# Loading only the 96 rows with data of r, k and w, from the fifth unit on

## The chip, the cores and the metric

The kernel runs on one core of a Trainium2 chip. Its time is the device time of one execution in microseconds (us). The kernel before takes 333.74 us, the median of three runs (333.08 to 336.19).

## The reference

Two layers follow each other: a linear attention with a decaying state (4 batches, 8 heads, 768 steps, head width 48), and a mixture of eight experts of which each token uses one (3072 tokens of width 384, hidden width 1024).

```python
for t in range(S):
    cur = np.einsum('bhd,bhe->bhde', u[None] * kt, vt)
    y[:, :, t] = np.einsum('bhd,bhde->bhe', rt, state + cur)
    state = wt[:, :, :, None] * state + np.einsum('bhd,bhe->bhde', kt, vt)
...
e_idx = np.argmax(x @ w_gate + modality_bias[modality_id], axis=1)
...
h = np.maximum(x[mask] @ w1[e], 0.0)
out[mask] = gate_w[mask, None] * (h @ w2[e])
```

## The kernel before, in words

**Units.** The attention is cut into 24 units (4 batches times 6 chunks of 128 steps); unit n is one chunk with its eight heads. Four heads' r, k and w stand on 64 partitions and the other four on the next 64. A head is only 48 wide, so of each 64 rows 48 hold data and 16 are padding. The host lays the padding out as 0 for r and k and 1.0 for w, and until now it is loaded with the rest: line 99 moves 128 rows, w (517 numbers a row, 2068 bytes) as one transfer and r with k (1024 numbers, 4096 bytes) as a second one. They go into one of four buffers, `ins[n % 4]`, called in0 to in3 in the listings. v has its own transfer (line 102, 128 rows of 2304 bytes).

**The work on a unit.** VectorE forms running products of the decay with two scans over 516 columns, B (line 296) and E (line 299), and writes four columns of w anew (line 298). GpSimd forms K (line 246) and G (line 307) from k and r, ScalarE copies r to PSUM (line 240), half_v (line 262) prepares v, and TensorE makes the products. In step i of the loop, units i+2, i+1 and i are at different stages (`att_iter`, line 288), every engine has the order of its work written out by hand, and unit i+6 is loaded into the buffer that unit i+2 has just left: its w may go once E of unit i+2 is done, its r and k once G and the copy of r are done. Lines 178 to 180 load the routing bias (bb) and the modality ids (mi, mi2) early; bb is read by VectorE at line 192. Steps 4 to 7 load pieces of expert weights (raw, line 223), steps 8 to 11 clear rows of a scratch tensor (xs, line 873), each of about the size of v's load.

**Queue and semaphores.** All these transfers are issued by SP, one after another. They announce their landing on eight semaphores that are taken in turn, called DMAHW0 to DMAHW7 in the listings. Before a transfer is issued, SP waits until the transfer that had the semaphore last, the eighth before it, has landed. So SP never has more than eight transfers under way.

**After the attention** come six blocks of 512 (or 416) tokens and a smaller one through the experts; the change touches nothing there. Lines 667 and 744, which the prediction uses for comparison, move four transfers of 32 rows each for a block, into and out of the chip's memory.

Of the kernel before, what the change touches and what calls it, by code (L numbers as in the profile page):

```python
# [17 lines left out]
B, H, S, D = 4, 8, 768, 48  # L18
P = 128
# [41 lines left out]
def kernel(ctx: ExitStack, tc: tile.TileContext, rkw, vt, wf, cst, mid, wg, bias, w1, w2, out):  # L61
    nc = tc.nc
# [22 lines left out]
    NIN = 4  # L85
    ins = [pa.tile([P, 1600], F32, name=f"in{i}", bufs=1) for i in range(NIN)]
# [9 lines left out]

    def load(n, cuts=((0, 1541),)):
        for c0, c1 in cuts:
            nc.sync.dma_start(out=ins[n % NIN][:, c0:c1], in_=rkw[n, :, c0:c1])

    def loadv(n):
        nc.sync.dma_start(out=wt(n, "v", [P, VW], 4), in_=vt[n * P:(n + 1) * P, :])
# [4 lines left out]
    nc.vector.memset(wm, 0.0)  # L107
    cs = cp.tile([P, NCST], F32, name="cs")
    load(0, ((1024, 1541), (0, 1024)))
    load(1, ((1024, 1541),))  # L110
    nc.sync.dma_start(out=cs[:, 256:NCST], in_=cst[:, 256:NCST])
    loadv(0)
    load(1, ((0, 1024),))
    nc.gpsimd.memset(cs[:, 0:2 * P], 1.0)
    for c0, op in ((0, ALU.is_equal), (P, ALU.is_gt)):
# [720 lines left out]
    for i in range(-2, NU):  # L836
# [39 lines left out]
        if i == NU - 3:  # L876
# [5 lines left out]
                                       in_=zt[:, None, :].to_broadcast([P, JT, XW])))  # L882
# [299 lines left out]
```

## Time and profile before

| what | value |
|---|---|
| median of three runs | 333.74 us |
| the profiled execution itself | 332.86 us |
| its span, first to last instruction | 331.1 us |
| busy over the span: TensorE, VectorE, ScalarE, GpSimd | 97%, 67%, 62%, 59% |
| moved by DMA | 66.22 MB, on average 200 GB/s |

Busy time is a mean over stages with different limits. In the page's 40 slices of 8.3 us each, VectorE shows 9 or 8 tenths in most of the first 13 slices (the attention, up to about 110 us) and much less behind them, while TensorE shows 9 nearly everywhere. A line such as "<-DMA in<-rkw" behind an idle time names what ended that idle time.

### The profile page before, as it was taken

Reading aid. Unit: us, or ns where it says so; the run is one execution under the profiler, and the core shown is the slowest. Engines: PE = TensorE matmul, PEld = TensorE weight load, DVE = VectorE, ACT = ScalarE, POOL = GpSimd, SP = SyncE. Lnnn points to the kernel's source line nnn. Section 1 sums busy time; section 2 is a strip of 40 time slices with the busy share of each in tenths; the row PEclk is TensorE's granted clock in tenths of the full one; section 3 lists DMA queues with packets and bytes.
Section 4 is the critical chain, followed back from the end, with each engine's and each line's share of the span. In section 5 each row is a group of like instructions: output and inputs, shape, how many; then the busy total and the mean of one; then the engine's idle time right before and its main releaser. Section 6 shows DMA issues by size and latency. Waiting matters only on the chain. (4 is left out here: it accounts for less than half of the span.)

```text
span 331.1 us, 9946 instructions
## 1 busy us (share of the span) xinstructions
PE 319.8 (97%) x3831; PEld 279.6 (84%) x3831; DVE 222.0 (67%) x382; ACT 204.0 (62%) x466; POOL 195.0 (59%) x226
## 2 busy tenths in 40 slices
PE   8899999999899999999999999999999999999993
PEld 3688999889799897888888888888888999889993
DVE  6999999899999746777514995874472465353220
ACT  3898799677588875642314748637775786524240
POOL 7998889879999975575435550652056233604041
PEclk9999999999999999999999999999999999999999
DMA  7998889967998532514778128945996594332011
GB/s 267 414 332 263 272 295 258 302 229 246 303 287 277 183 97 89 104 72 173 238 236 213 51 69 201 375 144 131 325 259 262 146 342 157 78 104 78 0 70 56
DMA packets 48321, 66.22 MB, mean 200 GB/s; under 512 B 27569, under 2 KB 34825, under 8 KB 48264
## 3 DMA queue, kind: packets, MB, share of 16 engines
q1 hardware_dynamic: 45160, 56.02, 55.0%
q0 software_dynamic: 3104, 9.47, 7.4%
q8 instruction: 32, 0.52, 0.6%
q14 instruction: 25, 0.20, 0.2%
HBM read 61.65 MB, written 16.46 MB: 236 GB/s over the span
## 5 line engine op out<-in xcount | busy, mean ns | idle before, releaser
L760 POOL DMA_INDIRECT out<-ot,xg x24 | 25.3, 1054 | 72.2 <-ACT ot L772 67.7
L228 ACT CAST wh<-raw 128x768 fp32r<-128x768 f32 x48 | 39.0, 830 | 32.3 <-PE pK_d L730 16.3
L229 POOL TENSOR_TENSOR wl<-raw,wh 128x768 fp32r<-128x768 f32 x20 | 38.8, 1953 | 28.5 <-ACT wh L228 28.4
L717 DVE SCALAR_TENSOR_TENSOR h<-pS_u,h 128x512 fp32r<-128x512 f32 (+1 forms) x34 | 22.9, 674 | 36.1 <-ACT h L716 30.9
L229 DVE TENSOR_TENSOR wl<-raw,wh 128x768 fp32r<-128x768 f32 x28 | 31.0, 1113 | 15.2 <-ACT wh L228 14.5
L711 PE MATMUL pS_u<-xh,wh 128*128 128x512 f32 (+1 forms) x102 | 39.7, 390 | 0.2 <-DVE h L717 0.2
L711 PE MATMUL pS_u<-xo,wh 128*128 128x512 f32 (+1 forms) x102 | 39.2, 384 | 0.0
L711 PE MATMUL pS_u<-xh,wl 128*128 128x512 f32 (+1 forms) x102 | 39.1, 384 | 0.0
L716 ACT ACTIVATE h<-pS_u 128x512 fp32r<-128x512 f32 (+1 forms) x34 | 19.8, 582 | 26.6 <-PE pS_u L711 22.5
L641 POOL DMA_INDIRECT xs<-xp,posT x24 | 24.5, 1022 | 11.2 <-issue 8.2
L246 POOL TENSOR_TENSOR K<-in,B 128x512 f32<-128x512 f32 x24 | 28.4, 1185 | 4.2 <-PE pK L321 2.3
L307 POOL TENSOR_TENSOR G<-in 128x512 f32<-128x512 f32 x24 | 30.6, 1274 | 0.0
L730 PE MATMUL pY_d<-h,wh 128*128 128x512 f32 (+1 forms) x80 | 30.5, 381 | 0.0
L730 PE MATMUL pX_d<-h,wh 128*128 128x512 f32 (+1 forms) x80 | 30.5, 381 | 0.0
L730 PE MATMUL pK_d<-h,wh 128*128 128x512 f32 (+1 forms) x80 | 30.5, 381 | 0.0
L296 DVE TENSOR_TENSOR_SCAN B<-in,pX_d 128x516 f32<-128x516 f32 x24 | 29.3, 1220 | 1.8 <-DMA in<-rkw 1.8
L299 DVE TENSOR_TENSOR_SCAN E<-in,pX_d 128x516 f32<-128x516 f32 x24 | 29.5, 1229 | 0.8
L386 PE MATMUL pY<-v,A 128*64 128x48 f32 x368 | 25.1, 222 | 0.0
L348 DVE TENSOR_TENSOR A<-pS,m 128x768 f32<-128x768 f32 x24 | 22.8, 948 | 2.9 <-PE pS L346 2.7
L252 ACT ACTIVATE pU_st<-pU_st,B 128x48 f32<-128x48 f32 x80 | 22.0, 275 | 3.0 <-PE pU_st L358 0.5
L386 PEld LDWEIGHTS pY<-v,A 128*64 128x64 f32 x368 | 23.7, 138 | 0.0
L346 PEld LDWEIGHTS pS<-R,K 64*64 64x64 f32 x768 | 18.6, 133 | 5.1 <-issue 4.2
(248 smaller groups left out, 829.6 us busy)
## 6 DMA issues: line engine op xcount, KB each, us to landing
raw<-w SPq DMA_DIRECT2D x24, 768.0 KB
in<-rkw SPq DMA_DIRECT2D x23, 512.0 KB
v<-vt SPq DMA_DIRECT2D x24, 288.0 KB
in<-rkw SPq DMA_DIRECT2D x23, 258.5 KB
wg<-wf SPq DMA_DIRECT2D x8, 576.0 KB
xl<-xs SPq DMA_DIRECT2D x20, 192.0 KB
raw<-w SPq DMA_DIRECT2D x16, 192.0 KB
yd<-yt SPq DMA_DIRECT2D x16, 192.0 KB
```

The costliest lines, as they stand in the source:

```text
L228: nc.scalar.copy(out=wh[k][:, sl], in_=raw[k][:, sl])
L229: (eng or (nc.vector, nc.gpsimd)[k]).tensor_tensor(out=wl[k][:, sl], in0=raw[k][:, sl], in1=wh[k][:, sl].bitcast(F32), op=ALU.subtract)
L246: nc.gpsimd.tensor_tensor(out=wt(a, "K", [P, 4, P]), in0=quarters(k), in1=quarters(T["B", a][:, 1:517])[:, :, 1:129], op=ALU.mult)
L296: nc.vector.tensor_tensor_scan(out=Bt[:, 516:0:-1], data0=w[:, 516:0:-1], data1=d1[:, 516:0:-1], initial=0.0, op0=ALU.mult, op1=ALU.max)
L299: nc.vector.tensor_tensor_scan(out=Et, data0=w[:, 0:516], data1=d1[:, 1:2].to_broadcast([P, 516]), initial=1.0, op0=ALU.mult, op1=ALU.max)
L307: nc.gpsimd.tensor_tensor(out=wt(a, "G", [P, 512]), in0=r, in1=k, op=ALU.mult)
L386: nc.tensor.matmul(out=yh[64:P, g, sw, hh], lhsT=A[:, hh, g, 1 + sw], rhs=vs[:, g, hh] if sw else v[:, h * D:(h + 1) * D], start=new and n ...
L641: rows_apart("xs", nc.gpsimd.indirect_dma_start(out=xs[:, :], out_offset=bass.IndirectOffsetOnAxis(ap=posT[:, n:n + 1], axis=0), in_=T["xp ...
L711: nc.tensor.matmul(out=pp, lhsT=wsrc[0][:, f, c * P:(c + 1) * P], rhs=xsrc[:, c], start=(n == 0), stop=(n == 3 * KC - 1))
L717: nc.vector.scalar_tensor_tensor(out=hl, in0=pp, scalar=0.0, in1=hh.bitcast(F32), op0=ALU.max, op1=ALU.subtract)
L730: nc.tensor.matmul(out=X["y", q][c][:, 0:width(q)], lhsT=wsrc[1][:, f, c * P:(c + 1) * P], rhs=hsrc, start=(first and n == 0), stop=(last ...
L760: ins = nc.gpsimd.indirect_dma_start(out=out[:, :], out_offset=bass.IndirectOffsetOnAxis(ap=xg[0:n, j, 1:2].bitcast(I32), axis=0), in_=ot[ ...
```

## The change

Units 0 to 3 load as before, all 128 rows, so each of the four buffers gets its padding once. From unit 4 on only rows 0 to 47 and rows 64 to 111 are loaded, each range as a transfer of its own; the padding from the buffer's first unit stays there.

```diff
     def load(n, cuts=((0, 1541),)):
         for c0, c1 in cuts:
-            nc.sync.dma_start(out=ins[n % NIN][:, c0:c1], in_=rkw[n, :, c0:c1])
+            for q in (slice(0, P),) if n < NIN else (slice(0, D), slice(64, 64 + D)):
+                nc.sync.dma_start(out=ins[n % NIN][q, c0:c1], in_=rkw[n, q, c0:c1])
```

One line is added, so every later line's number grows by one. Line 99's two transfers for a unit become four for each of units 4 to 23. On SP, where units 4 to 6 are loaded, this stood before (the target, its source, rows x numbers a row, and the semaphores that SP waits for first):

```order
L99 DMA in0_94<-rkw 128x517 [waits DMAHW3_49,DVE_49]
L99 DMA in0_94<-rkw 128x1024 [waits DMAHW4_49,Activation_49,Pool_49]
L99 DMA in1_95<-rkw 128x517 [waits DMAHW5_49,DVE_49]
L99 DMA in1_95<-rkw 128x1024 [waits DMAHW6_49,Activation_49,Pool_49]
L102 DMA v3_363<-vt 128x576 [waits DMAHW7_49]
L99 DMA in2_96<-rkw 128x517 [waits DMAHW0_49,DVE_49]
L99 DMA in2_96<-rkw 128x1024 [waits DMAHW1_49,Activation_49,Pool_49]
L178 DMA bb_139<-bias 128x16 [waits DMAHW2_49]
L179 DMA mi_140<-mid 24x256 [waits DMAHW3_49]
L180 DMA mi2_163<-mid 24x256 [waits DMAHW4_49]
```

The first row is w of unit 4, the second its r and k. A transfer takes the semaphore that it waited for: w of unit 4 takes DMAHW3, and mi waits for its landing. In the changed kernel the same stretch reads:

```order
L100 DMA in0_94<-rkw 48x517 [waits DMAHW3_49,DVE_49]
L100 DMA in0_94<-rkw 48x517 [waits DMAHW4_49]
L100 DMA in0_94<-rkw 48x1024 [waits DMAHW5_49,Activation_49,Pool_49]
L100 DMA in0_94<-rkw 48x1024 [waits DMAHW6_49]
L100 DMA in1_95<-rkw 48x517 [waits DMAHW7_49,DVE_49]
L100 DMA in1_95<-rkw 48x517 [waits DMAHW0_49]
L100 DMA in1_95<-rkw 48x1024 [waits DMAHW1_49,Activation_49,Pool_49]
L100 DMA in1_95<-rkw 48x1024 [waits DMAHW2_49]
L103 DMA v3_367<-vt 128x576 [waits DMAHW3_49]
L100 DMA in2_96<-rkw 48x517 [waits DMAHW4_49,DVE_49]
L100 DMA in2_96<-rkw 48x517 [waits DMAHW5_49]
L100 DMA in2_96<-rkw 48x1024 [waits DMAHW6_49,Activation_49,Pool_49]
```

Eight semaphores now reach back over little more than one and a half units instead of nearly three. v3 waits for the first half of unit 4's w, and behind these rows bb waits for DMAHW0, the second half of unit 5's w.

On GpSimd, where K of unit 4 is made, the instruction waits for three semaphores before:

```order
L303 TENSOR_TENSOR dV2_480<-v2_199,dT2_434 128x384 [waits DMAHW2_49,Activation_49,Pool_49]
L246 TENSOR_TENSOR K4_482<-in0_94,B4_475 128x512 [waits DMAHW4_49,DVE_49,PE_49]
L307 TENSOR_TENSOR G4_484<-in0_94 128x512 [waits PE_49]
L421 TENSOR_TENSOR xp0_388<-xp0_388,dV1_382 128x384 [waits Activation_49]
L194 TENSOR_TENSOR ec_167<-ec_167,cs_100 128x16 [waits DMAHW3_49,DVE_49]
```

and for four in the changed kernel, one for each of the two transfers of r and k:

```order
L304 TENSOR_TENSOR dV2_488<-v2_199,dT2_440 128x384 [waits DMAHW2_49,Activation_49,Pool_49]
L247 TENSOR_TENSOR K4_490<-in0_94,B4_483 128x512 [waits DMAHW5_49,DMAHW6_49,DVE_49,PE_49]
L308 TENSOR_TENSOR G4_492<-in0_94 128x512 [waits PE_49]
L422 TENSOR_TENSOR xp0_394<-xp0_394,dV1_388 128x384 [waits Activation_49]
L195 TENSOR_TENSOR ec_167<-ec_167,cs_100 128x16 [waits DMAHW3_49,DVE_49]
```

The order of the work on GpSimd, ScalarE, VectorE and TensorE is otherwise the same; only the waits for r, k and w name two transfers where they named one.

## Rows read from the trace of the kernel before

**Rows 1.** Windows: stretch, its length, busy us by engine (instructions), clock, DMA share, GB/s.
```profile
5.00:20.00 15.00, 13.06 (x280) 9.93 (x278) 14.66 (x19) 11.56 (x36) 13.47 (x22) 1.00 1.03 400
20.00:110.00 90.00, 87.59 (x2252) 81.02 (x2250) 86.22 (x122) 71.92 (x220) 80.32 (x86) 1.00 0.86 273
```

**Rows 2.** Tile in: count, ns min/median/max, first and last start; idle ended by it (us, times).
```profile
L99 SPq DMA_DIRECT2D in<-rkw x47: 327/328/1282, 0.8 to 94.5; - x47
L296 DVE TENSOR_TENSOR_SCAN B<-in,pX_d x24: 1216/1219/1228, 3.7 to 108.2; 128x516 f32<-128x516 f32 x24
...
  DMA in<-rkw: 5.9, 4
```

**Rows 3.** Timeline of POOL: start, us, what, [idle before <-releaser].
```profile
8.52 1.19 POOL L246 TENSOR_TENSOR K<-in,B 128x512 f32<-128x512 f32 x1 [0.94 <-DMA in<-rkw]
```

**Rows 4.** DMA issues: line's transfer, queue, count, KB each.
```profile
in<-rkw SPq DMA_DIRECT2D x23, 512.0 KB
v<-vt SPq DMA_DIRECT2D x24, 288.0 KB
in<-rkw SPq DMA_DIRECT2D x23, 258.5 KB
raw<-w SPq DMA_DIRECT2D x16, 192.0 KB
```

**Rows 5.** Timeline of SP around unit 11's load.
```profile
36.25 0.33 SPq L99 DMA_DIRECT2D in<-rkw  x1
36.78 0.34 SPq L223 DMA_DIRECT2D raw<-w  x1
37.32 0.33 SPq L99 DMA_DIRECT2D in<-rkw  x1
```

**Rows 6.** Timeline of DVE: scan B of unit 11, which reads that load.
```profile
51.20 1.22 DVE L296 TENSOR_TENSOR_SCAN B<-in,pX_d 128x516 f32<-128x516 f32 x1
```

**Rows 7.** Waits of SP's queue: who waited, for whom, us, times, longest.
```profile
SPq L99 <- DVE E L299: 20.5, 17, 2.2
SPq L99 <- POOL G L307: 15.7, 13, 2.4
...
SPq L99 <- DMA in<-rkw: 1.5, 3, 0.8
```

**Rows 8.** Timeline of SP: issue of v3, mi, and unit 7's r and k.
```profile
11.34 0.44 SPq L102 DMA_DIRECT2D v<-vt  x1
...
16.46 0.44 SPq L179 DMA_DIRECT2D mi<-mid  x1
...
19.72 1.28 SPq L99 DMA_DIRECT2D in<-rkw  x1
```

**Rows 9.** Timelines of ACT and DVE: first readers of v3 and of bb.
```profile
22.27 0.72 ACT L262 COPY vz<-v 64x192 f32<-64x192 f32 x2
...
23.38 0.16 DVE L192 TENSOR_REDUCE emx<-bb 128x2 f32<-128x16 f32 x1
```

**Rows 10.** Timeline of SP: four 32-row loads, and four 32-row stores.
```profile
134.22 1.97 SPq L667 DMA_DIRECT2D xl<-xs  x4
...
161.96 2.04 SPq L744 DMA_DIRECT2D yd<-yt  x4
```

**Rows 11.** Windows of 0.25 us while those loads, then those stores, run.
```profile
136.25:136.50 0.25, 0.25 (x3) 0.21 (x2) 0.25 (x2) 0.13 (x1) 0.04 (x1) 1.00 1.06 283
163.00:163.25 0.25, 0.25 (x3) 0.19 (x2) 0.25 (x1) 0.00 (x0) 0.15 (x1) 1.00 0.89 212
```

**Rows 12.** Lines 246 and 240: wait instructions on the queues of POOL and ACT.
```profile
L246 POOLq EVENT_SEMAPHORE  x24: 17/1237/2517, 4.9 to 107.4; - x24
...
L240 ACTq EVENT_SEMAPHORE  x23: 17/38/38, 8.4 to 110.1; - x23
```

## The prediction, made before the changed kernel ran

> **What bounds the kernel now.** The change works between the first load of unit 4 and the last load at 94.5 us [rows 2], so I read the attention alone, first by windows. From 20 to 110 us VectorE is busy 86.22 of 90 us and TensorE 87.59; the DMA engines are 0.86 busy and move 273 GB/s [rows 1]. High shares on three sides do not say which one holds the others back, so the next view is what ended the idle times. Transfers of r, k and w ended four idle times, 5.9 us in all [rows 2], and the last of them ended at 8.52 us, before K of unit 1 [rows 3]. In the waits of 20 to 115 us no transfer stands. So no engine waits for a load that the change makes smaller; the compute engines set the pace, one unit every (108.2 - 3.7) / 23 = 4.54 us [rows 2], and the loads follow the buffers: SP's own long waits at line 99 are for E (20.5 us) and G (15.7 us) to release a buffer [rows 7].
>
> How far ahead the loads are is seen on unit 11. Its w is issued at 36.25 us and read at 51.20 us, 15 us later [rows 5, 6].
>
> The one stretch where DMA is scarce is 5 to 20 us, at share 1.03 and 400 GB/s [rows 1]. There the eight semaphores already bind: 1.5 us of SP's waits at line 99 are for the landing of r, k and w [rows 7]. That is where I look for harm.
>
> **The change part by part.**
>
> *Bytes removed.* 32 rows of 6164 bytes in 20 units are 3.95 MB. At 400 GB/s [rows 1] that is 9.9 us of DMA time. Nobody waits for it, so it is worth 0. The bound from the other side: if all of VectorE's idle time from 20 to 110 us were owed to DMA traffic in some way that no wait shows, 90 - 86.22 = 3.8 us could come back.
>
> *Issues added.* Two more per unit, 40 in all. With nothing to wait for, SP issues every 0.53 us (36.25, 36.78, 37.32) [rows 5], so a unit needs at most six issues, 3.2 us of 4.54, where four needed 2.1. The added 21 us lie in the 36 us in which SP waited for E and G anyway [rows 7]. A later r and k by about 1 us meets a lead of 15 us. Price 0; what covers it is that lead.
>
> *Less reach of the semaphores, steady part.* SP now waits for a landing that was issued about 1.5 units, some 6 us, earlier (with a raw or xs transfer 1.3 units). A unit is 199 + 393 kB of r, k and w, 295 kB of v and at times 197 kB of raw or xs (from the rows' KB, [rows 4]): 1.08 MB, 2.7 us at 400 GB/s. The traffic fits well into 4.54 us, so a wait here can be short only, and the lead takes it. Price 0.
>
> *Less reach, at 5 to 20 us.* Here the lead is smallest. Two readers are near. v3 is read at 22.27 us and bb at 23.38 us [rows 9]; v3 was issued at 11.34 us [rows 8], and landed before 19.72 us, since unit 7's r and k wait for its semaphore [rows 8]. Now v3 may go only when the first half of unit 4's w has landed, and bb when the second half of unit 5's w has. The whole w of unit 4 had landed by 16.46 us, when mi got its semaphore [rows 8]; I take that as the latest time. Behind it lie, up to unit 5's w, 99 + 393 + 199 = 691 kB: 1.7 us at 400 GB/s, so bb is issued at 18.2 us at the latest. Ahead of it in the engines then stand r and k of unit 5, v3, and unit 6: 393 + 295 + 199 + 393 = 1280 kB, 3.2 us. bb lands by 21.4 us, 2.0 us early. v3, by the same count, has 1084 kB ahead and 295 of its own: 16.46 + 3.4 = 19.9 us, 2.4 us early. Price 0.
>
> This used 400 GB/s for transfers of 48 rows, of which the trace has none. The nearest rows are transfers of 32 rows [rows 10]: the loads reach 283 GB/s, the stores 212 [rows 11], both with pieces of 384 bytes, where ours have 2068 and 4096. Bounds therefore are 400 and 212 GB/s. At 212 a steady unit takes 2.8 + 0.74 + 0.49 = 4.0 us, still under 4.54. But bb: 16.46 + 691/212 + 985/212 + 0.74 = 25.1 us, 1.7 us late on VectorE. I take the upper half, as small pieces and not few rows may explain 283: price 0, upper end +1.7. The limit is 273 GB/s; below it bb is late.
>
> *Waits added.* K waits for two landings instead of one, as do B and the copy of r in most units. A wait instruction whose semaphore is long reached takes 17 ns on GpSimd's queue and 38 on ScalarE's [rows 12]. Twenty of each on the path would be 1.1 us. But the queues stand ahead of their engines here (the median wait before K is 1237 ns, [rows 12]) and neither engine sets the pace: 80.32 and 71.92 of 90 us busy [rows 1]. Price 0, upper end +1.1.
>
> *Behind the attention.* 40 more transfers are five rounds of eight semaphores, so later transfers wait for the same ones as before. 0.
>
> **The sum.** 332.86 us (span 331.1 and 1.8 around it) + 0. That execution lies 0.9 us below the median of 333.74; against the median I forecast **333.7 us**, no change. One per cent, 3.3 us, is about what a measurement of this kernel tells from no change.
>
> **The rivals.**
>
> *Narrow transfers are slow, bb comes late.* At the stores' 212 GB/s this gives 333.7 + 1.7 = 335.4 us. For it: the stores [rows 11]. Against it: the loads' 283, above the limit of 273 though in small pieces, and that 16.46 was taken as latest. [...]
>
> *Each half takes as long as the whole did.* Then w takes 0.66 us and r with k 1.31 us for every half (265 and 524 kB at 400 GB/s), a unit 3.9 + 0.74 + 0.49 = 5.2 us, more than 4.54. bb would land at 16.46 + 4.6 + 7.3 = 28.4 us, 5.0 us late: **338.7 us**, slower. After that the lead would just hold (8 units with a raw or xs transfer lose 0.6 us each, 12 others 0.15: 6.9 us of 15). It would exceed 1% from 177 GB/s downwards, (691 + 985) kB in 9.5 us. Against it stand both rates of the narrow rows.
>
> *Less traffic frees the engines.* All of 3.8 us comes back: 329.9 us. Nothing in the waits speaks for it.
>
> That the smaller loads are not made is excluded: the listing of SP shows transfers of 48 rows.
>
> **Chances.** Forecast 0.78 (0.01 of it beyond 1% on either side), late bb 0.12 (0.01 beyond 1%), halves as long as wholes 0.06, traffic relief 0.04. Faster by over 1%: 0.04 + 0.01 = 0.05. Slower: 0.06 + 0.01 + 0.01 = 0.08. Within: 0.87. The range takes in the two upper ends, 333.7 + 1.7 + 1.1 = 336.5, and below half of VectorE's idle time, 333.7 - 1.9 = 331.8; the halves as long as wholes and full relief stay outside.
>
> **What would show it.** Right: VectorE's B scans still 4.54 us apart, no idle time after 9 us ended by r, k, w, v or bb, SP's waits at line 100 shifted from E and G to landings, about 62 MB moved. Wrong: line 193 waiting for bb near 23 us (first rival), idle times before half_v or B in steady units (second), a shorter scan spacing (third). The forecast fails if a transfer of 48 rows runs below 273 GB/s, or if VectorE's instructions themselves depend on DMA traffic.

## The result, and the profile after

The changed kernel takes 336.65 us (median of 16 runs, 334.53 to 342.36) against 333.28 us for the kernel before beside it (16 runs, 332.48 to 336.35): a ratio of 1.0088, 95% interval 1.0065 to 1.0110. Ratios are taken from fast executions alone, while the medians include a few slow ones, so a ratio is not the quotient of the medians. A second series gave 336.07 against 333.76, 1.0061 (1.0019 to 1.0103). I had forecast 333.7 us and no change, in a range of 331.8 to 336.5; it is slower by 0.6 to 0.9%, the first median just above the range and the second inside it. The profiled execution took 334.53 us, span 332.8; it is the fastest of the 16.

Fewer bytes went through the DMA engines and took as long as before: the queue of these transfers moved 56.02 MB in 55.0% of 16 engines' span before and 52.08 MB in 55.5% now. Windows of the changed kernel, in the columns of [rows 1]:

```profile
5.00:20.00 15.00, 12.21 (x258) 9.25 (x259) 14.50 (x19) 10.63 (x32) 12.80 (x22) 1.00 0.99 317
15.00:20.00 5.00, 3.48 (x92) 3.05 (x92) 4.93 (x7) 4.65 (x16) 4.94 (x10) 1.00 0.92 229
20.00:110.00 90.00, 88.46 (x2275) 81.74 (x2271) 85.69 (x122) 72.70 (x223) 79.66 (x85) 1.00 0.90 241
```

From 15 to 20 us the same window of the kernel before reads:

```profile
15.00:20.00 5.00, 4.17 (x109) 3.82 (x109) 4.93 (x7) 4.64 (x16) 4.68 (x9) 1.00 1.05 401
```

So 229 GB/s at a share of 0.92 stand against 401 at 1.05: while 48-row transfers prevail, the rate is 0.57 of what it was, and for a full share 0.65 (249 against 382 GB/s). TensorE's busy time in these five microseconds fell from 4.17 to 3.48 us. From 20 to 110 us the share rose from 0.86 to 0.90 while the rate fell from 273 to 241 [rows 1].

The loads themselves (tile in; count, ns, first and last start, and the idle time that they ended) answer to [rows 2]:

```profile
L100 SPq DMA_DIRECT2D in<-rkw x87: 310/385/2182, 0.8 to 96.3; - x87
L297 DVE TENSOR_TENSOR_SCAN B<-in,pX_d x24: 1219/1219/1229, 3.7 to 108.5; 128x516 f32<-128x516 f32 x24
...
  DMA in<-rkw: 8.3, 5
```

The last of the five ends at 9.76 us, ahead of unit 1's K; none is in the steady part. The scans stand (108.5 - 3.7) / 23 = 4.56 us apart, 4.54 before. SP waits less for E and G and more for landings ([rows 7]; who waited, for whom, us, times, longest):

```profile
SPq L100 <- POOL G L308: 11.1, 6, 2.4
...
SPq L100 <- DMA in<-rkw: 6.1, 9, 2.5
SPq L100 <- DMA v<-vt: 3.9, 6, 0.9
...
SPq L100 <- DVE E L300: 2.7, 3, 1.3
```

bb, the first rival's load, goes out at 19.45 us instead of 15.37, and VectorE waits 0.37 us for it. Timeline of SP, then of VectorE, of the changed kernel:

```profile
19.45 0.42 SPq L179 DMA_DIRECT2D bb<-bias  x1
```

```profile
22.81 0.96 DVE L349 TENSOR_TENSOR A<-pS,m 128x768 f32<-128x768 f32 x1 [0.56 <-PE pS L347]
...
24.73 0.17 DVE L193 TENSOR_REDUCE emx<-bb 128x2 f32<-128x16 f32 x1 [0.37 <-DMA bb<-bias]
24.94 0.17 DVE L194 TENSOR_TENSOR ec<-bb,emx 128x16 f32<-128x16 f32 x1
25.03 1.22 DVE L297 TENSOR_TENSOR_SCAN B<-in,pX_d 128x516 f32<-128x516 f32 x1
```

Ahead of it VectorE waited 0.56 us for TensorE, and that wait was in none of my cases. It hides a part of bb's lateness: VectorE comes to bb later, and so waits less for it. The wait of 0.56 us begins with a pause of TensorE inside one group of 16 equal matmuls. Timeline of TensorE, kernel before, then changed kernel:

```profile
16.87 0.34 PE L277 MATMUL pT<-cs,G 128*64 128x2 f32 x5
17.55 0.46 PE L277 MATMUL pT<-cs,G 128*64 128x2 f32 x10 [0.34 <-issue]
```

```profile
18.48 0.46 PE L278 MATMUL pT<-cs,G 128*64 128x2 f32 x10 [1.04 <-issue]
```

"issue" says that TensorE waited for nothing that the profile shows. Five of the 16 equal matmuls had already run, so a late operand is an unlikely cause. The profile's DMA queues hold a candidate: one that carries instructions. In the changed kernel (packets, MB, share of 16 engines):

```profile
q1 hardware_dynamic: 44520, 52.08, 55.5%
...
q8 instruction: 32, 0.52, 0.7%
```

That is 32 blocks of 16.4 kB in 332.8 us. By windows of 0.1 us the block ahead of the pause starts between 15.0 and 15.1 us in the kernel before, and between 15.7 and 15.8 in the changed one:

```profile
q8 instruction: 1, 0.02, 61.6%
```

```profile
q8 instruction: 1, 0.02, 78.4%
```

The share of 16 engines gives its duration: 0.616 x 1.6 = 0.99 us, and 0.784 x 1.6 = 1.25 us. The pause ends about 1.5 us after the block has come in (16.0 to 16.1 and 17.55; 17.0 and 18.48). The other pauses bear this out: of the 62 pauses of TensorE of 0.3 us or more that the profile puts down to issue between 4 and 120 us, in the 18 traces of this text, 61 end 1.24 to 1.74 us after such a block has come in; the last, of 0.30 us in bb_first, ends 3.31 us after one. So my theory, for which the experiments follow: TensorE stands at a border of its code, and the next block, which the page counts to the same 16 DMA engines as the loads, is held up by the narrow transfers. The pauses that this is to explain are 0.30 to 2.44 us each.

### The profile page after: what moved, and what is told of

Its sections match the earlier page's. It is cut to its first block, busy times and chain, and to the rows that moved or that the text cites. A ratio compares the mean times of both kernels' runs of the same rounds, so it can differ in the third digit from the quotient of the medians.

```text
span 332.8 us, 10019 instructions
## 1 busy us (share of the span) xinstructions
PE 320.1 (96%) x3830; PEld 279.8 (84%) x3831; DVE 221.4 (67%) x382; ACT 204.4 (61%) x466; POOL 195.1 (59%) x226
## 2 busy tenths in 40 slices
DMA packets 47681, 62.27 MB, mean 187 GB/s; under 512 B 28209, under 2 KB 35465, under 8 KB 47624
## 3 DMA queue, kind: packets, MB, share of 16 engines
q1 hardware_dynamic: 44520, 52.08, 55.5%
## 5 line engine op out<-in xcount | busy, mean ns | idle before, releaser
L300 DVE TENSOR_TENSOR_SCAN E<-in,pX_d 128x516 f32<-128x516 f32 x24 | 29.5, 1229 | 0.8
L712 PEld LDWEIGHTS pS_u<-xh,wh 128*128 128x128 f32 x102 | 19.1, 188 | 4.2 <-DVE h L718 0.9
```

Source lines behind the costliest of these rows:

```text
L300: nc.vector.tensor_tensor_scan(out=Et, data0=w[:, 0:516], data1=d1[:, 1:2].to_broadcast([P, 516]), initial=1.0, op0=ALU.mult, op1=ALU.max)
L712: nc.tensor.matmul(out=pp, lhsT=wsrc[0][:, f, c * P:(c + 1) * P], rhs=xsrc[:, c], start=(n == 0), stop=(n == 3 * KC - 1))
```

## The experiments

Ratios are to the kernel before on the same chip: 333.76 us (35 runs) beside again_1, cols, from_8 and bb_first, 334.09 (17) beside first_4, rows112, halves and pe_shift, 334.38 (35) beside the two shifts, from_8_again and from_8_shift. "Pauses" are the sum of TensorE's idle times of 0.3 us or more put down to issue between 4 and 120 us of the profiled execution; the clock is the median over the runs of their mean granted clock (for the kernel before, over the 35 runs beside again_1).

| kernel | us | ratio (95%) | GB/s and share, 15 to 20 us | pause at 17 us | pauses, us | clock |
|---|---|---|---|---|---|---|
| before | 333.28 | 1 | 401, 1.05 | 0.34 | 1.86 | 0.997 |
| changed | 336.65 | 1.0088 (1.0065-1.0110) | 229, 0.92 | 1.04 | 2.42 | 0.9915 |
| again_1 | 336.07 | 1.0061 (1.0019-1.0103) | 242, 1.05 | 1.56 | 3.27 | 0.993 |
| cols | 333.99 | 1.0009 (0.9970-1.0048) | 340, 0.98 | 0.34 | 1.33 | 0.9975 |
| bb_first | 336.14 | 1.0063 (1.0028-1.0098) | 244, 0.98 | none | 2.42 | 0.9915 |
| from_8 | 333.34 | 0.9965 (0.9929-1.0001) | 391, 1.04 | none | 2.08 | 0.997 |
| first_4 | 336.58 | 1.0093 (1.0052-1.0133) | 255, 1.06 | 1.44 | 3.60 | 0.992 |
| rows112 | 340.39 | 1.0172 (1.0108-1.0236) | 275, 1.05 | 1.26 | 5.02 | 0.986 |
| halves | 347.51 | 1.0396 (1.0338-1.0453) | 265, 1.03 | 1.55 | 8.79 | 0.9885 |
| shift_timed | 335.85 | 1.0060 (1.0026-1.0094) | 209, 0.88 | none | 1.13 | 0.997 |
| before_shift | 336.32 | 1.0080 (1.0047-1.0113) | 405, 1.05 | none | 2.25 | 0.997 |
| from_8_again | 333.95 | 1.0005 (0.9969-1.0042) | 393, 1.04 | none | 0.36 | 0.9975 |
| from_8_shift | 334.47 | 0.9997 (0.9961-1.0034) | 407, 1.05 | none | 2.26 | 0.998 |

The sums of the pauses do not order the times: the kernel before has 1.86 us of them, shift_timed 1.13 us, and shift_timed is slower. So the pauses are not the whole account.

**again_1: the changed kernel, unchanged.**

> The changed kernel once more, unaltered, for a second trace and a second set of times. Theory A (narrow: a transfer of 48 rows moves at about half the rate of 128 rows, so the loads of units 4 to 7, v3 and bb come late while the DMA engines are full): 336 to 338 us, ratio to before 1.007 to 1.012, 180 to 240 GB/s at a full DMA share between 13 and 20 us, where before has 400, and VectorE idle for bb near 24 us. Theory B (count: twice as many transfers share the eight semaphores and SP's issues): the same time, so this run does not tell A from B. What it is to show is where a granted clock below 0.99 lies, if one is there.

The loss is there again, 1.0061, and so is the pause, longer this time:

```profile
18.71 0.46 PE L278 MATMUL pT<-cs,G 128*64 128x2 f32 x10 [1.56 <-issue]
```

Here it can be seen that the block is late and not TensorE. Ahead of the pause TensorE takes up the same work at the same time, in the kernel before and then in again_1:

```profile
15.49 0.63 PE L321 MATMUL pK<-cs,K 128*128 128x128 f32 x4 [0.60 <-DVE R L243]
```

```profile
15.43 0.63 PE L322 MATMUL pK<-cs,K 128*128 128x128 f32 x4 [0.60 <-DVE R L244]
```

Yet the block starts between 15.9 and 16.0 us instead of between 15.0 and 15.1, and takes 1.28 us (a share of 0.801 of 1.6) instead of 0.99. first_4 shows the same, with a start in the same tenth of a microsecond. The wait for bb that I had expected near 24 us is not in again_1's trace: the longer pause of TensorE covers it.

**cols: all 128 rows, each transfer cut in two by columns.**

```diff
-            nc.sync.dma_start(out=ins[n % NIN][:, c0:c1], in_=rkw[n, :, c0:c1])
+            mid = (c0 + c1) // 2
+            for d0, d1 in ((c0, c1),) if n < NIN else ((c0, mid), (mid, c1)):
+                nc.sync.dma_start(out=ins[n % NIN][:, d0:d1], in_=rkw[n, :, d0:d1])
```

> All 128 rows from unit 4 on, padding too, but each transfer cut in two by columns, so that SP issues as many transfers as in the changed kernel, in the same places and with the same waits. Theory A: the rate at 5 to 20 us stays near 400 GB/s, bb is in time, time as before (ratio 0.998 to 1.003, 333 to 334 us). Theory B: as the changed kernel, ratio 1.006 to 1.012, 335.5 to 337.5 us.

1.0009 with the changed kernel's number of transfers. Not with all of its waits, as I had expected: the cut by columns falls between r and k, so K, which reads k alone, waits for one landing as before (24 wait instructions at its line, 42 in the changed kernel). The rate of the thin stretch nearly holds, and the pause is that of before:

```profile
5.00:20.00 15.00, 12.69 (x279) 9.88 (x277) 14.65 (x19) 11.56 (x35) 13.47 (x22) 1.00 1.01 375
```

```profile
17.58 0.46 PE L279 MATMUL pT<-cs,G 128*64 128x2 f32 x10 [0.34 <-issue]
```

So neither the 40 issues nor the shorter reach of the eight semaphores makes the loss: those prices of 0 stand, within an interval that ends at 1.0048.

**from_8: narrow only from unit 8 on.**

```diff
-            for q in (slice(0, P),) if n < NIN else (slice(0, D), slice(64, 64 + D)):
+            for q in (slice(0, P),) if n < 2 * NIN else (slice(0, D), slice(64, 64 + D)):
```

> The narrow transfers begin with unit 8 instead of unit 4. If the harm is done in the first 25 us, where the lead of the loads is small: ratio 0.998 to 1.003. If narrow transfers or their number cost something in every unit: at least 16/20 of the change's loss, ratio 1.006 or more.

0.9965, interval up to 1.0001. Sixteen of the 20 narrow units are still there, and the loss is gone: it comes from units 4 to 7, loaded in the thin stretch. These 16 units also have the added waits (38 wait instructions at K's line), so the waits make no loss there.

**bb_first: the changed kernel, with bb and the ids loaded before unit 4.**

```diff
+    early()
...
-        if i == 0:
-            early()
```

> The changed kernel, but bb and the two loads of modality ids are issued before unit 4's loads instead of behind unit 6's. If the late bb is the whole loss: ratio 0.999 to 1.004. If v3, w and r with k are late too and hold up other engines: ratio 1.004 or more, with idle time before half_v, B or K between 7 and 25 us.

1.0063: with bb in time the loss stays. In its trace the pause at 17 us is missing too, but a longer one stands at the next place. TensorE's timeline, then windows (the clock is the third number from the end), then VectorE:

```profile
29.57 0.34 PE L359 MATMUL pU_st<-v,KT 128*48 128x48 f32 x7 [1.70 <-issue]
```

```profile
27.90:29.50 1.60, 0.00 (x0) 0.00 (x0) 1.56 (x5) 0.21 (x2) 0.34 (x3) 1.00 1.03 235
...
29.80:33.20 3.40, 3.40 (x58) 3.40 (x53) 1.79 (x3) 2.21 (x8) 3.32 (x5) 0.51 0.89 204
```

```profile
33.59 0.56 DVE L424 TENSOR_TENSOR xp<-pY,dV 128x384 f32<-128x384 f32 x1 [1.93 <-PE pY L387]
```

TensorE does nothing from 27.9 to 29.5 us; then its granted clock is 0.51 for 3.4 us, and VectorE waits 1.93 us for it. Unit 7's scan B starts at 36.34 us, in the kernel before at 33.53. So the pause of 1.70 us and the drop behind it cost 2.8 us here.

**first_4: narrow for units 4 to 7 alone.**

```diff
-            for q in (slice(0, P),) if n < NIN else (slice(0, D), slice(64, 64 + D)):
+            for q in (slice(0, P),) if not NIN <= n < 8 else (slice(0, D), slice(64, 64 + D)):
```

> Narrow transfers for units 4 to 7 alone, whole transfers again from unit 8. Theory C (narrow rows in the crowded stretch make TensorE's next piece of code late): the whole loss is here, ratio 1.005 to 1.009, an idle of TensorE put down to issue of 1.0 us or more between 15 and 31 us, and 5 to 20 us at 310 to 340 GB/s; from 40 us on the rates of before. Theory S (the narrow transfers of the later units cost as much): half of the loss, 1.003 or less.

1.0093, the whole loss, from four units. Its pause at 17 us:

```profile
18.60 0.46 PE L278 MATMUL pT<-cs,G 128*64 128x2 f32 x10 [1.44 <-issue]
```

**rows112: from unit 4 on one transfer of rows 0 to 111.**

```diff
-            for q in (slice(0, P),) if n < NIN else (slice(0, D), slice(64, 64 + D)):
+            for q in (slice(0, P),) if n < NIN else (slice(0, 64 + D),):
```

> From unit 4 on one transfer of rows 0 to 111 in place of two of 48 rows (16 rows of padding stay in it, and before's count of transfers). Theory N (a transfer that lies on one half of the partitions moves at half the rate, one that spans both halves does not): 5 to 20 us at 380 to 410 GB/s, no longer idle of TensorE by issue than 0.4 us at 17 us, ratio 0.997 to 1.001. Rival F (any transfer of fewer than 128 rows is slow): below 350 GB/s and 1.004 or more.

A miss, and the most useful one. With before's number of transfers, and 16 rows less in each, the rate falls to 275 GB/s and the time grows by 1.7%. The windows also show the clock after its pause:

```profile
15.00:20.00 5.00, 3.27 (x79) 2.97 (x81) 4.93 (x7) 4.01 (x13) 4.67 (x9) 0.91 1.05 275
...
17.00:18.50 1.50, 0.24 (x7) 0.15 (x6) 1.50 (x2) 1.46 (x4) 1.50 (x2) 1.00 1.05 263
...
19.30:22.50 3.20, 3.20 (x44) 3.11 (x41) 2.63 (x4) 1.74 (x7) 3.12 (x4) 0.50 1.08 267
```

```profile
24.33 0.96 DVE L349 TENSOR_TENSOR A<-pS,m 128x768 f32<-128x768 f32 x1 [2.33 <-PE pS L347]
```

TensorE was busy 0.24 of 1.5 us, then ran at clock 0.50, and VectorE waited 2.33 us at the place where it waited 0.56 us in the changed kernel, whose clock stayed at 1.00 there. The pauses were 1.26 and 1.04 us, so most of the difference comes with the drop.

**halves: all 128 rows, cut into rows 0 to 63 and 64 to 127.**

```diff
-            for q in (slice(0, P),) if n < NIN else (slice(0, D), slice(64, 64 + D)):
+            for q in (slice(0, P),) if n < NIN else (slice(0, 64), slice(64, P)):
```

> From unit 4 on all 128 rows, cut in two by rows (0 to 63, 64 to 127): the count of transfers of the changed kernel and the bytes of the kernel before. Theory N: half the rate with all the bytes, so 5 to 20 us at 320 GB/s or less, 20 to 110 us at a DMA share above 0.95, and worse than the changed kernel, ratio 1.008 to 1.03. Rival P (it was the missing padding or the 48 rows, not the cut by halves): as the cut by columns, 0.997 to 1.005 and 375 GB/s.

1.0396, beyond the 1.03 that I had allowed: the bytes of before, the count of cols, and the largest loss of the kernels that were timed more than once. What differs from cols is the cut, by rows instead of by columns, and the waits for a second landing. Its longest pause:

```profile
42.00 0.55 PE L372 MATMUL pY<-SPb,R 128*64 128x96 f32 x8 [2.44 <-issue]
```

**pe_shift: the changed kernel, each warm-up matmul cut in two, which puts 36 more TensorE instructions ahead of everything.**

```diff
-        for i in range(n):
-            nc.tensor.matmul(out=wp, lhsT=wm[:, 0:P], rhs=wm, start=(i == 0), stop=(i == n - 1))
+        for i in range(2 * n):
+            nc.tensor.matmul(out=wp[:, 0:256], lhsT=wm[:, 0:P], rhs=wm[:, 0:256], start=(i == 0), stop=(i == 2 * n - 1))
```

> The changed kernel with each warm-up matmul of 512 columns cut into two of 256: 36 more TensorE instructions ahead of 17 us, the same columns. Theory C (TensorE stands at a border between two pieces of its code): the idle put down to issue at 17 to 18 us leaves the 6th of the 16 matmuls of line 278 and lies 36 instructions earlier, inside the 32 matmuls of line 347, after about the 19th (16th to 22nd). Rival D (that matmul waits for data that a load or another engine brings): it stays ahead of the 6th matmul of line 278.

One run, 335.74 us. The pause did not move to line 347 as expected: it vanished. The 16 weight loads of line 278, cut at five in the others, run through, and the block of instructions now starts at 12.0 us (a window from 11.95 to 12.05):

```profile
16.84 0.55 PEld L278 LDWEIGHTS pT<-cs,G 128*64 128x64 f32 x16
```

```profile
q8 instruction: 1, 0.02, 57.9%
```

With the border 36 instructions earlier the block was fetched 3.7 us sooner, while the engines still moved 388 GB/s (12 to 13 us; from 14 to 15 us it is 209). So the pause hangs on the place in the code and not on a load of data, and the block is TensorE's. The time of this one run is no better for it: VectorE now waits 0.80 us for bb.

**shift_timed, before_shift and from_8_shift: the same edit, timed, in the changed kernel, in the kernel before and in from_8. from_8_again: from_8 once more.**

> The changed kernel with the 36 added TensorE instructions, timed. Theory C (the loss of the changed kernel is TensorE's idle for its next piece of code at 17 to 18 us and the drop of the granted clock that follows it in some executions): no issue idle of 0.3 us or more before 40 us, mean granted clock back to 0.996 (median) and ratio 1.000 to 1.004. Theory C-many (such an idle comes at whichever border meets the crowded queue, so moving one border moves the loss): an idle of 0.4 us or more elsewhere and 1.004 to 1.009. Rival D (late data): 1.006 to 1.009 with the idle at 17 us unchanged.

> The kernel before with the same 36 TensorE instructions added. Theory C: the 0.34 us of idle at 17 us goes, and where no other border is hit the time is that of before or up to 0.3% less, 0.997 to 1.001. Rival (the added instructions cost something themselves): above 1.002, and then the timed shift of the changed kernel has to be read against this one.

> The kernel with whole rows up to unit 7 and narrow transfers from unit 8 on, a second time. If the first result (0.9965) was no chance: 0.993 to 0.999; if the bytes saved are worth nothing and the stalls of single executions even out: 0.999 to 1.002.

> Whole rows up to unit 7, narrow from unit 8, with the 36 added TensorE instructions. Theory C: as the better of the two it is made of, 0.993 to 1.000, with no issue idle above 0.3 us before 35 us; the narrow transfers of units 8 to 12 (40 to 60 us) can still hold a border's code back by 0.4 to 1.8 us, as in the profiled execution without the shift.

The shift took the pause at 17 us away and brought the changed kernel's clock back to 0.997, as expected, but not its time: 1.0060. Its trace shows a reason. VectorE, no longer held up by TensorE, now waits 1.31 us for bb, and unit 5's scan B starts at 24.99 us, as late as in the changed kernel (25.03). In the kernel before it starts at 24.20. VectorE in the kernel before, in shift_timed, and in from_8_shift, where bb is in time:

```profile
24.20 1.22 DVE L296 TENSOR_TENSOR_SCAN B<-in,pX_d 128x516 f32<-128x516 f32 x1
```

```profile
24.69 0.17 DVE L193 TENSOR_REDUCE emx<-bb 128x2 f32<-128x16 f32 x1 [1.31 <-DMA bb<-bias]
...
24.99 1.22 DVE L297 TENSOR_TENSOR_SCAN B<-in,pX_d 128x516 f32<-128x516 f32 x1
```

```profile
24.17 1.22 DVE L297 TENSOR_TENSOR_SCAN B<-in,pX_d 128x516 f32<-128x516 f32 x1
```

So in the traces the late code and the late bb are two routes of the same delay, and each hides behind the other. The shift takes away one, bb_first the other, and the loss stays each time. A kernel without both was not run.

before_shift, where I had expected no loss, is slower too: 1.0080. Its trace is of the slowest of its 12 executions, and it shows a pause followed by a drop of the clock:

```profile
83.65 0.56 PE L346 MATMUL pS<-R,K 64*64 64x128 f32 x15 [1.17 <-issue]
```

```profile
84.40:88.00 3.60, 3.60 (x75) 3.60 (x73) 3.53 (x5) 1.89 (x7) 3.41 (x4) 0.58 0.92 288
```

Behind the attention TensorE also waits 0.96 us for VectorE near 200 us, in before_shift and in shift_timed, and not in the kernel before. But the shift does not always cost: from_8_shift takes as long as the kernel before, 0.9997, though its trace has a pause of 1.23 us at 32.8 us, where I had expected none above 0.3.

What narrow transfers for units 4 to 7 cost with the shifted code is read from shift_timed against from_8_shift, which differ in nothing else: 335.85 against 334.47 us in the same series; the means of their 12 runs each lie 2.0 us apart (95% interval 0.8 to 3.2). That is the loss of the unshifted kernels, 2.3 to 3.4 us by their medians, or a little less. Against before_shift, 336.32 us, shift_timed shows no loss at all; but before_shift is the one kernel with whole transfers for units 4 to 7 that is measurably slower than the kernel before, and why is not known. from_8_again, 1.0005, says that from_8's 0.9965 was mostly chance: 197 kB less per unit (32 rows of 6164 bytes) from unit 8 on are worth nothing that can be measured in the unshifted code.

**rows120, rows96, mid64, low64: one transfer of rows 0 to 119, 0 to 95, 32 to 95 and 0 to 63 from unit 4 on, one run each.** What was open: whether any transfer of fewer than 128 rows is slow, or one that lies on one half of the partitions.

```diff
-            for q in (slice(0, P),) if n < NIN else (slice(0, D), slice(64, 64 + D)):
+            for q in (slice(0, P),) if n < NIN else (slice(32, 96),):
```

> One transfer of rows 0 to 119 per cut from unit 4 on. Theory W (only a transfer of all 128 rows goes at full rate, since a smaller one is spread over the 16 DMA engines in rows that no longer fall apart evenly): 15 to 20 us at 270 to 320 GB/s with a share of about 1, close to the 275 of 112 rows. Theory L (the rate falls in step with the rows): 340 to 390 GB/s.

> One transfer of rows 0 to 95 from unit 4 on (rows 96 to 127 of these units keep older data, so the output is not the reference's; read for rates alone). Theory W: 250 to 290 GB/s between 15 and 20 us, as 112 rows. Theory L: 240 or less.

> One transfer of rows 32 to 95 from unit 4 on, 32 rows of each half of the partitions (the other rows keep older data; read for rates alone). Theory H (a transfer on one half of the partitions is the slow one): 330 GB/s or more between 15 and 20 us. Theory W: 300 or less, as rows 0 to 63.

> One transfer of rows 0 to 63 from unit 4 on, all on the lower half of the partitions (the other rows keep older data; read for rates alone). Theories H and W: 220 to 280 GB/s between 15 and 20 us while its transfers run; only against rows 32 to 95 does it tell them apart.

The edit shown is that of mid64. Windows from 15 to 20 us, of rows120, rows96, mid64 and low64:

```profile
15.00:20.00 5.00, 3.06 (x84) 2.77 (x86) 4.93 (x7) 3.88 (x13) 4.70 (x9) 1.00 0.97 245
```

```profile
15.00:20.00 5.00, 3.38 (x74) 3.09 (x75) 4.93 (x7) 3.65 (x12) 4.73 (x10) 0.78 1.05 262
```

```profile
15.00:20.00 5.00, 4.38 (x110) 4.04 (x111) 4.93 (x7) 4.64 (x16) 4.71 (x10) 1.00 0.74 213
```

```profile
15.00:20.00 5.00, 2.51 (x71) 2.22 (x72) 4.93 (x7) 3.54 (x11) 4.70 (x9) 1.00 1.06 211
```

With the same 64 rows' worth of bytes, rows 32 to 95 need a share of 0.74 and rows 0 to 63 need 1.06 for the same 212 GB/s or so: 288 against 199 GB/s per full share, where 128 rows give 382. By the words of my expectation 213 GB/s speak for theory W, but they left the engines idle for a quarter of the time, so the rate alone does not decide. In this stretch the position seems to count, in one trace each; from 20 to 110 us the two need nearly the same share, 0.69 and 0.71, for 198 and 199 GB/s. mid64 has no pause at 17 us (331.65 us, against 332.31 for the kernel before beside these four) where low64 has one of 1.99 us. (low64's own time, 402.13 us, tells nothing: with stale rows it does other work behind the attention, and loads expert weights 28 times for 24.) But a span over both halves isn't enough: 96, 112 and 120 rows run at 245 to 275 GB/s, and 120 rows, 94% of the bytes, took 346.51 us.

Per full share the rate was 382 GB/s with 128 rows, 288 with rows 32 to 95, 262 with rows 0 to 111 (275 at 1.05), 249 with the two times 48 rows and 199 with rows 0 to 63. That is not the order of the row counts: 64 rows in the middle go ahead of 112. No run here shows which DMA engine moved which rows, so the cause stays open, and the uneven spread over the engines in my expectation for 120 rows was not shown.

## Why the prediction was wrong, point by point

- **The step that failed** is the rate in the thin stretch: "I take the upper half, as small pieces and not few rows may explain 283: price 0". With 48-row transfers for units 4 to 7 the engines moved 199 (pe_shift) to 255 GB/s (first_4) between 15 and 20 us, below the limit of 273 that I had named (271 when the sum is done again), and around the 212 of the stores that I had kept as the lower end. "Small pieces" could not be told from "few rows" in that trace, and I chose the reading that cost nothing.
- **The first rival had the cause right and half of the path.** The rate fell and bb came late: at 24.7 us in the changed kernel and in shift_timed, where the rival's sum gave 25.1. With the pause out of the way VectorE waits 1.31 us for it (the rival: 1.7). But with bb in time the loss was the same (bb_first, 1.0063), and that is the half that was in no sum of mine: TensorE's code, a block of which is held up by about a microsecond. My search for readers of a late transfer listed v3 and bb and not the engines' instructions, though the pause stood in the trace of before with 0.34 us, and the instruction queue on its page. That the range's upper end, 336.5 us, nearly takes in the measured 336.65 is luck: it adds bb's lateness to 1.1 us of wait instructions that cost nothing, and leaves the code out.
- **The size.** In the two profiled executions of the changed kernel the clock held at 17 us and spans were 1.7 and 1.8 us longer. In the first, unit 5's scan B is 0.8 us late; the last scan is only 0.3 us late, since the kernel before has a pause of 0.96 us of its own at 84 us; a pause of 1.06 us at 114 us follows. The median run lost more: its mean granted clock is 0.9915 (0.993 in the second series) against 0.997. In stretches at half clock (0.50 and 0.51 in the windows of rows112 and bb_first) that is 2 x 0.0055 x 335 = 3.7 us (2.7), about one stretch as in bb_first. But the clock is the smaller part: the seven of the 16 runs with a clock of 0.994 or more have a median of 335.36 us, 2.1 us above the kernel before, and the other nine 337.09. How often a pause is followed by a drop I cannot say; it was in rows112 and bb_first, and not after the 1.04 and 1.56 us at 17 us above.
- **Prices of 0 that held:** the issues and the semaphores' reach as far as the compute engines' own loads go (cols, 1.0009); the added waits (from_8, 0.9965); the bytes removed, which nobody waited for (from_8_again, 1.0005). SP's waits moved from E and G to landings, and 62.27 MB were moved, as said.
- **K's waits.** The row that answers to [rows 12] in the changed kernel: 

```profile
L247 POOLq EVENT_SEMAPHORE  x42: 17/43/2516, 4.9 to 107.7; - x42
```

18 wait instructions more. from_8 and from_8_again have 14 more and no loss.
- **Halves as long as wholes** (second rival): a half has 48 of 128 rows, 0.375 of the bytes, at 0.57 of the rate (229 of 401), so it took about 0.66 of the whole's time in the thin stretch, and the two halves together 1.3 times as long as the whole. The lead did not run down: B's spacing was 4.56 us, and the scans waited for no load in steady units.
- **A reading of the trace of before** that was not quite so: in its waits of 20 to 115 us one transfer does stand, v, for which GpSimd waited 0.2 us at line 641. It changes nothing in the sum.

What is shown: the loss is made by units 4 to 7 (from_8 0.9965, first_4 1.0093, and with shifted code shift_timed against from_8_shift, 2.0 us), and by the cut along rows, not by the count (cols 1.0009, halves 1.0396). TensorE's pauses go with the blocks of the instruction queue (61 of 62), and the one at 17 us with the place in the code (pe_shift, where it is gone and the block starts at 12.0 instead of 15.7 us). What is not shown is how the loss divides between the late code and the late bb, since no kernel was run without both. That the narrow transfers delay the block inside the DMA engines is argued from its later start at the same progress of TensorE and its longer duration; no run showed the queue inside an engine. Why the shift alone costs the kernel before 0.8%, and from_8 nothing, is not known.

## What to carry to other kernels

Price a transfer by what rows it covers, and not by its bytes: here, with 3/4 of the bytes of r, k and w from unit 4 on, the queue of the loads took as much of the DMA engines' time as with all of them (55.5% of 16 engines' span against 55.0%), and of the shapes tried only full 128-row transfers kept the rate or nearly (401 GB/s whole, 340 cut by columns, 275 at most with fewer rows). Where the DMA share is about 1, count the engines' own instructions among the transfers that may come late: here a block of them started 0.7 us later in the changed kernel and 0.9 in again_1, and took 1.25 and 1.28 us instead of 0.99. Look for idle times put down to issue that stand inside a run of equal instructions, and compare kernels with shifted code before a loss of under 1% is put down to an edit: here the shift alone moved one kernel by 0.8% and another not at all. When two things are late at about the same time, taking away one shows little; take away each and both. Where the loads were 15 us ahead, the bytes saved were worth nothing that could be measured (from_8_again, 1.0005).

## What the runs showed of the hardware

- The queue that the page calls instruction moved 32 blocks of 16.4 kB in 332.8 us (changed kernel), 0.7% of the span of 16 DMA engines. With 36 more TensorE instructions ahead of it the block of 15.7 us started at 12.0 us (pe_shift). Of TensorE's 62 pauses of 0.3 us or more put down to issue between 4 and 120 us in 18 traces, 61 ended 1.24 to 1.74 us after a block had come in. The longest was 2.44 us (halves).
- With transfers of 120 or 112 rows in place of 128 the DMA engines moved 245 and 275 GB/s between 15 and 20 us instead of 401, at shares of 0.97 and 1.05 against 1.05.
- After a pause of 1.17 to 1.70 us TensorE's granted clock was 0.50 to 0.58 over the windows of 3.2 to 3.6 us behind them in three traces (rows112, bb_first, before_shift), and stayed at 1.00 after one of 1.56 us in again_1 and one of 1.64 us in from_8.
